# Reordering the steps of a hand-scheduled attention stage ahead of a mixture of experts

## The chip, the cores and the metric

The kernel runs on one core of a Trainium2 chip. The metric is the device time of one execution in microseconds (us); lower is better. The engines are named as in the profile: PE multiplies matrices (PEld is its weight load), DVE and ACT work element by element, POOL issues the indirect transfers, SP issues most of the others.

## The reference, cut to what matters

```python
f = 1.0 / (1.0 + np.exp(-f_logit))               # (4, 8, 768, 48): batch, heads, time, width
for t in range(768):
    state = f[:, :, t, :, None] * state + k[t] (outer) v[t]      # 48 x 48 per batch and head
    y[:, :, t] = q[t] @ state
x = y as (3072 tokens, 384)
g = argmax(x @ w_group);  e = argmax(x @ w_expert[g])            # 4 groups of 4 experts
out = softmax weight of g * softmax weight of e * (relu(x @ w1[g, e]) @ w2[g, e])   # F = 1024
```

Each token goes to one of 16 experts. All numbers are fp32.

## The kernel before, in words

The time axis is cut into 6 chunks of 128 steps, each chunk into 2 **units** of two batches: unit i = (chunk i // 2, half s = i % 2), 12 units (NU). Inside a chunk the recurrence is done by matrix products. A unit goes through **stages**, each a Python generator whose pieces end at a `yield`; the letter is the one that the written order uses:

- c `bounded` (L519): DVE keeps the logits f above -44.
- g `gated`: ACT computes Exp and Ln of f (L529, L530; one piece), then for each of the two batches PE forms the running sums `cs` by a triangular matrix (L536) and ACT makes `eq` and `kh` from them (L537, L538); the last row of `eq`, the chunk's decay, is copied to the tile `ends` by a transfer that ACT issues (L543).
- m `multiplied`: DVE multiplies q by eq (L551) and k by kh (L554).
- t `turned`: PE transposes q and k (L566), ACT copies them out (L567); a fifth piece, in odd units, transposes `ends` to `gt` on PE (L573), and ACT copies that to `decays` (L574).
- s `scored`: PE computes the scores `ap` (L587), DVE masks them to `am` (L590).
- n `stated`: PE computes the state's increment `ds` (L604); in a second piece DVE adds it to the state and multiplies by the decays (L610, L611).
- w `weighed`: PE multiplies q by the state (L626); second piece: the scores by v (L631), and ACT copies the outputs to `xT` (L634).
- d `done`: PE forms the router's logits `lT`, ACT copies them (L646, L648); second piece: PE turns them (`lg`, L651), DVE copies them (L652); after an odd unit the routing of the chunk starts.
- x `listed`: two pieces transpose the outputs (`x_ps`, L666) and copy them (L667), a third issues their store to `x_dram` from ACT's queue (L669).
- r is a slot for one piece of the routing (`route`): the first two find the best group and expert (ranks, DVE), the third counts tokens per expert on PE (`rk`, L204), the fourth takes each token's place from it (pick, L213 to L216), the next three prepare tables and weights, then PE makes a table of tokens by place (`tb`, L251) and DVE adds it up (L255). After chunk 3 `ranking` (L270 to L283) also picks the two early experts, whose weights are loaded and whose tokens are fetched at once. After chunk 5 it ranks all 16.
- e is a slot for one piece of the early experts' work (`early`): transposing their tokens (L399), 8 pieces of their first layer (L409), 2 of their second (L431).
- l loads the inputs of a unit: SP issues four transfers of 384 KB (L513).

The order on PE, DVE and ACT is the order in which the pieces are issued, written out by hand: a list BEGIN for the first units, then one list per **step** i from 3 on (EVEN or ODD, or one of ORDERS), where `t` is unit i, `g+1` unit i + 1, `d-2` unit i - 2. A piece that a generator no longer has is skipped. SP and POOL are ordered by a planner. Input tiles of f and k have 2 buffers, qh 3, v 4; all products share 8 PSUM banks.

After step NU, 14 main passes of up to 230 tokens and, first and last, one of 128 run their two layers on PE (`turn_in` L399, `up` L409, `down` L438, `turn_out` L447), each with 3 MB of weights; DVE and ACT copy, POOL fetches the tokens (L386) and scatters the results (L423).

Of the kernel before, what the change touches and what calls it, by code (L numbers as in the profile page):

```python
# [22 lines left out]
def kernel(  # L23
# [12 lines left out]
    nc = tc.nc  # L36
# [42 lines left out]
    def bank(shape, name):  # L79
        return ps.tile(shape, FP32, tag="bank", name=name)  # L80
# [98 lines left out]
    def route(c, lg, sb, tabled=True, tidy=None, ranking=None):  # L179
# [68 lines left out]
        if tabled:  # L248
            tb = bank([P, 2, GE, 2], "tb")
            for b in range(B):  # L250
                nc.tensor.matmul(tb.rearrange("p m e j -> p m (e j)"), lhsT=ln[:, b], rhs=val[:, :, b, :], start=(b == 0), stop=(b == B - 1))  # L251
            if ranking:
                ranking(sb)
                yield
            nc.vector.tensor_tensor(table, table, tb, OP.add)  # L255
# [209 lines left out]
    with ExitStack() as fast:  # L465
# [27 lines left out]
        NU = len(units)  # L493
# [28 lines left out]
        def gated(i):  # L522

            c, s = units[i]
            w = live[i]

            nl = w["f"].rearrange("p b h d -> p b (h d)")
            for b in parts(i):
                nc.scalar.activation(nl[:, b], nl[:, b], AF.Exp, bias=0.0, scale=-1.0)  # L529
                nc.scalar.activation(nl[:, b], nl[:, b], AF.Ln, bias=1.0, scale=1.0)  # L530
            eq, qh, kh = pads["eq"][i % 2], w["qh"], pads["kh"][i % 3]
            w.update(eq=eq, kh=kh)
            yield
            for b in range(2):
                cs = bank([P, H, D], "cs")
                nc.tensor.matmul(cs.rearrange("t h d -> t (h d)"), lhsT=tri, rhs=nl[:, b], start=True, stop=True)  # L536
                nc.scalar.activation(eq[:, b, :, 0:D], cs, AF.Exp, bias=0.0, scale=-1.0)  # L537
                nc.scalar.activation(kh[:, b, :, 0:D], cs, AF.Exp, bias=0.0, scale=1.0)  # L538
                if b:

                    if s == 0:
                        ends[c] = sb.tile([B, H * DP], FP32, tag="ends", bufs=1, name="ends")
                    nc.scalar.dma_start(out=ends[c][2 * s:2 * s + 2, :], in_=eq[P - 1:P].rearrange("o b h d -> o b (h d)"))  # L543
                yield
# [12 lines left out]
        def turned(i):  # L557
            w = live[i]
            w["g"] = decays[:, units[i][0], :, 2 * units[i][1]:2 * units[i][1] + 2].rearrange("p a b -> p b a")
            for nm in ("q", "k"):  # L560
                w["T" + nm] = sb.tile([P, 2, HP, P], FP32, tag="T" + nm, name="T" + nm)
            for b in range(2):
                for nm in ("q", "k"):
                    pt = bank([P, HP, P], "tr_" + nm)
                    for a in range(HP):
                        nc.tensor.transpose(out=pt[:, a, :], in_=w[nm + "h"][:, b, 2 * a:2 * a + 2, :].rearrange("t r d -> t (r d)"), identity=ident)  # L566
                    (nc.vector.tensor_copy if i == 0 and nm == "k" else nc.scalar.copy)(w["T" + nm][:, b], pt)  # L567
                    yield
            c, s = units[i]
            if s:  # L570
                gt = bank([P, HP, B], "gt")
                for a in range(HP):
                    nc.tensor.transpose(out=gt[:, a, :], in_=ends[c][:, a * P:(a + 1) * P], identity=ident[0:B, 0:B])  # L573
                nc.scalar.copy(decays[:, c], gt)  # L574
            yield
# [108 lines left out]
        def advance(gens):  # L684
# [5 lines left out]

        STAGES = {"c": bounded, "g": gated, "m": multiplied, "t": turned, "s": scored, "n": stated, "w": weighed, "d": done, "x": listed}
        BEGIN = """c0 g0 p g0 g0 m0 m0 m0 m0 l2 t0 t0 t0 t0 c1 g1 s0 s0 s0 s0 g1 g1 p w0 w0 n0 m1 m1 m1 m1 l3 h x0 x0 x0
            t1 t1 t1 t1 t1 c2 g2 s1 s1 s1 s1 p d0 g2 g2 n0 n1 w1 w1 m2 m2 l4 n1
            d0 x1 x1 x1 t2 t2 t2 t2 c3 g3 s2 s2 s2 s2 g3 g3 w2 d1 w2 n2 m3 m3""".split()
        BEGUN = 3
        EVEN = "l+2 d-2 r r r x-1 x-1 x-1 t t t t g+1 g+1 r n-1 c+2 s s s s w g+2 d-1 w n m+1 m+1".split()
        ODD = "l+2 d-2 r r x-1 x-1 x-1 t t t t g+1 g+1 t r n-1 c+2 r s s s s w g+2 d-1 w n m+1 m+1 n".split()

        ORDERS = {
            4: "l+2 d-2 r r r x-1 x-1 x-1 t t t t g+1 g+1 r n-1 s s s s w d-1 w n m+1 m+1 c+2 g+2".split(),
            5: "l+2 d-2 r r x-1 x-1 x-1 t t t t g+1 g+1 t r n-1 r s s s s w d-1 w n m+1 m+1 n c+2 g+2".split(),
            3: "l+2 d-2 r r x-1 x-1 x-1 t t t t c+1 g+1 g+1 g+1 t r n-1 r s s s s w d-1 w n m+1 m+1 n c+2 g+2".split(),
            NU - 2: "d-2 r r r x-1 x-1 x-1 t t t t g+1 g+1 r n-1 s s s s w d-1 w r n m+1 m+1".split(),
            NU: "d-2 e r r x-1 x-1 x-1 d-1 d-1 r r r e r e r r r r e e e r r e e e r e e".split(),
        }
        steps_of = {}

# [187 lines left out]
    with tc.If(more > 0), ExitStack() as late:  # L897
# [5 lines left out]
        with tc.For_i(0, last, 1) as i:  # L903
            w1, w2 = load_weights(wp, b_expert[0:1, bass.ds(i, 1)])
# [13 lines left out]
            w = fetch(ep, row, P)  # L918
# [32 lines left out]
```

## Time and profile before

| | us |
|---|---|
| runs: median of 3 (lowest to highest) | 466.87 (464.18 to 467.26) |
| the profiled execution | 463.0 |
| its span, first to last instruction | 461.1 |
| PE busy | 433.4 (94% of the span) |
| DVE busy | 175.5 (38%) |
| ACT busy | 122.4 (27%) |
| POOL busy | 74.7 (16%) |

The granted clock of PE is 0.995 of full speed over the span. Busy time of PE counts the modelled ends of pipelined matmuls. Attention and routing fill the first 160 us or so, the experts the rest; the shares above are means over both.

### The profile page before, as it was taken

What the parts mean: (1) busy time and instruction counts of PE and PEld (TensorE: products, weight loads), DVE (VectorE), ACT (ScalarE), POOL (GpSimd) and SP (SyncE); (2) the same over time, 40 slices, a digit from 0 to 9 for tenths busy, and PEclk for the clock granted to TensorE, in tenths of its full rate; (3) what the DMA queues carried; (4) which work ended last, traced back from release to release, by engine and by line L of the source; (5) the groups of instructions that cost most, each with busy time, mean ns of one, the idle gap of its engine ahead of it and who ended that gap; (6) DMA issues with size and microseconds to landing.
All of it is one profiled execution on the core that took longest, in us unless ns stands there. A gap on an engine that the chain in (4) does not pass through costs nothing.

```text
span 461.1 us, 9310 instructions
## 1 busy us (share of the span) xinstructions
PE 433.4 (94%) x3875; PEld 401.5 (87%) x3875; DVE 175.5 (38%) x464; ACT 122.4 (27%) x265; POOL 74.7 (16%) x107
## 2 busy tenths in 40 slices
PE   4999799899999999999999999999999999999991
PEld 2888678788888886989999999999999999999980
DVE  6665474758588670211047121120220221122110
ACT  5565466566655321000101101001011001001000
POOL 3000000000002007311022131312122211120120
PEclk9999999999999999999999999999999999999998
DMA  9999999997706919977538367376486486464100
GB/s 167 174 197 202 202 200 186 194 173 142 138 36 217 390 48 328 309 278 283 174 127 299 102 244 246 110 296 217 128 305 211 137 300 233 129 253 146 42 29 17
DMA packets 136187, 87.71 MB, mean 190 GB/s; under 512 B 106692, under 2 KB 127258, under 8 KB 136138
## 3 DMA queue, kind: packets, MB, share of 16 engines
q1 hardware_dynamic: 126754, 72.38, 60.0%
q0 software_dynamic: 6016, 9.87, 6.6%
q10 hardware_dynamic: 3368, 4.80, 3.2%
q8 instruction: 32, 0.52, 0.5%
q14 instruction: 17, 0.14, 0.1%
HBM read 77.50 MB, written 9.83 MB: 189 GB/s over the span
## 4 chain that ended last, share of the span: by engine, by line
PE 80%; DVE 7%; ACT 5%; DMA 3%; issue 1%; SPq 1%; ACTq 0%; POOL 0%; POOLq 0%; DVEq 0%
PE hp L409 29%; PE yo L438 25%; PE yo L431 4%; PE y L631 4%; DVE am L590 3%; PE ap L587 2%; PE xg_ps L399 2%; PE y_ps L447 2%; PE cs L536 2%; PE ds L604 2%; PE x_ps L666 2%; PE tr_k L566 1%; DMA ld_k<-in_k_dram 1%; PE lT L646 1%; DMA x_dram<-blank 1%
## 5 line engine op out<-in xcount | busy, mean ns | idle before, releaser
L409 PE MATMUL hp<-xe,w 128*128 128x128 f32 (+14 forms) x864 | 138.8, 320 | 1.5 <-issue 0.8
L409 PEld LDWEIGHTS hp<-xe,w 128*128 128x128 f32 x864 | 135.7, 190 | 2.5 <-issue 1.0
L438 PE MATMUL yo<-h,w 128*128 128x230 f32 (+13 forms) x672 | 116.9, 334 | 0.0
L438 PEld LDWEIGHTS yo<-h,w 128*128 128x128 f32 x672 | 113.0, 190 | 0.5
L411 DVE TENSOR_SCALAR h<-hp 128x256 f32<-128x256 f32 (+14 forms) x32 | 17.8, 556 | 129.7 <-PE hp L409 129.7
L423 POOL DMA_INDIRECT out_dram<-yt,xg x32 | 34.6, 1081 | 168.5 <-DVE yt L422 112.4
L439 ACT COPY yT<-yo 128x230 f32<-128x230 f32 (+13 forms) x28 | 9.1, 327 | 145.9 <-PE yo L438 145.9
L413 ACT ACTIVATE h<-hp 128x256 f32<-128x256 f32 (+14 forms) x40 | 18.8, 469 | 102.5 <-PE hp L409 102.5
L386 POOL DMA_INDIRECT xg<-x_dram,rows_p x30 | 32.3, 1078 | 70.2 <-DVE rows_p L322 25.0
L590 DVE TENSOR_TENSOR am<-ap,tri 128x512 f32<-128x512 f32 x48 | 29.8, 681 | 6.1 <-PE ap L587 6.0
L536 PE MATMUL cs<-ld_f,tri 128*128 128x384 f32 x48 | 19.5, 532 | 10.6 <-ACT ld_f L530 10.6
L439 DVE COPY yT<-yo 128x230 f32<-128x230 f32 (+13 forms) x14 | 5.1, 367 | 62.9 <-issue 38.9
L631 PE MATMUL y<-am,v 128*64 128x128 f32 x384 | 26.1, 276 | 2.8 <-DVE am L590 2.7
L631 PEld LDWEIGHTS y<-am,v 128*64 128x64 f32 x384 | 22.1, 137 | 5.7 <-DVE am L590 5.0
L587 PE MATMUL ap<-Tq,Tk 48*128 48x128 f32 x384 | 25.0, 280 | 1.6 <-ACT Tk L567 1.5
L587 PEld LDWEIGHTS ap<-Tq,Tk 48*128 48x128 f32 x384 | 22.7, 187 | 2.7 <-ACT Tk L567 2.0
L536 PEld LDWEIGHTS cs<-ld_f,tri 128*128 128x128 f32 x48 | 8.6, 200 | 15.4 <-ACT ld_f L530 6.8
L431 PE MATMUL yo<-w,h 128*128 128x384 f32 x64 | 21.2, 487 | 0.0
L245 POOL COPY meta<-token 128x4 int32<-128x4 int32 x6 | 1.9, 320 | 114.2 <-DMA x_dram<-meta 114.2
L431 PEld LDWEIGHTS yo<-w,h 128*128 128x128 f32 x64 | 11.9, 190 | 7.7
L634 ACT COPY xT<-y 128x512 f32<-128x512 f32 x24 | 12.9, 589 | 20.7 <-PE y L631 20.7
L422 DVE TENSOR_SCALAR yt<-y_ps,xg 128x384 f32<-128x384 f32 (+14 forms) x28 | 15.8, 606 | 6.4 <-PE y_ps L447 6.4
(166 smaller groups left out, 428.9 us busy)
## 6 DMA issues: line engine op xcount, KB each, us to landing
w<-in_moe_w_dram SPq DMA_DIRECT2D x34, 1536.0 KB, 9.5
qh<-in_q_dram SPq DMA_DIRECT2D x12, 384.0 KB, 6.4
ld_k<-in_k_dram SPq DMA_DIRECT2D x12, 384.0 KB, 6.7
v<-in_v_dram SPq DMA_DIRECT2D x12, 384.0 KB, 6.6
x_dram<-x ACTq DMA_DIRECT2D x12, 384.0 KB, 5.0
ld_f<-in_f_logit_dram SPq DMA_DIRECT2D x11, 384.0 KB, 5.4
out_dram<-yt,xg POOLq DMA_INDIRECT x32, 3.8
xg<-x_dram,rows_p POOLq DMA_INDIRECT x30, 6.9
```

The source lines that it names most:

```text
L386: nc.gpsimd.indirect_dma_start(out=w["x"][0:m, j, :], out_offset=None, in_=x_dram[0:1 + top, :], in_offset=bass.IndirectOffsetOnAxis(ap=ro ...
L409: nc.tensor.matmul(hp[:, o, :], lhsT=w1[:, ko, (f + o) * P:(f + o + 1) * P], rhs=w["xT"][:, ko, :], start=(ko == 0), stop=(ko == KO - 1))
L411: nc.vector.tensor_scalar(h[:, f:f + 2, :], hp, 0.0, None, OP.max)
L413: nc.scalar.activation(h[:, f:f + 2, :], hp, AF.Relu)
L422: nc.vector.tensor_scalar(y[0:m], yp[0:m], w["x"][0:m, j, DM:DM + 1], None, OP.mult)
L423: nc.gpsimd.indirect_dma_start(out=out, out_offset=bass.IndirectOffsetOnAxis(ap=w["x"][0:m, j, DM + 1:RW].bitcast(U32), axis=0), in_=y[0:m ...
L431: nc.tensor.matmul(yp, lhsT=w["h"][:, fo, :], rhs=w2[:, fo, :], start=(fo == 0), stop=(fo == FO - 1))
L438: nc.tensor.matmul(yp, lhsT=w2[:, fo, m * P:(m + 1) * P], rhs=w["h"][:, fo, :], start=(fo == 0), stop=(fo == FO - 1))
L536: nc.tensor.matmul(cs.rearrange("t h d -> t (h d)"), lhsT=tri, rhs=nl[:, b], start=True, stop=True)
L587: nc.tensor.matmul(ap[r][:, a, :], lhsT=w["Tk"][rows, b, a, :], rhs=w["Tq"][rows, b, a, :], start=True, stop=True)
L590: nc.vector.tensor_tensor(am[:, r], ap[r], tri.unsqueeze(1).broadcast_to((P, HP, P)), OP.mult)
L631: nc.tensor.matmul(ys[r][DP * b:DP * b + DP, a, :], lhsT=w["v"][:, b, 2 * a + r, :], rhs=w["am"][b][:, r, a, :], start=(c == 0 and a == 0) ...
```

## The change

Most of it is in the written order. The fifth piece of `turned` becomes a stage of its own, b (`decayed`), and stands at the begin of odd steps, followed by the second piece of n of the unit before. The bound c+2 stands behind the scores' masks. Exp and Ln become two pieces (for units after the first): Exp stands behind lT's copy, Ln behind the copies of the outputs. The third piece of x, the store, stands behind the running sums of the next unit. In odd steps the fourth r stands at the end. The orders of steps 3, 4 and 5 are dropped, so that these follow ODD and EVEN, and BEGIN ends with c4, Exp and Ln of unit 4. `ranking` has a piece of its own, and the slots of steps 10 and 12 are rearranged for it. One copy of turned keys in unit 0 goes from DVE to ACT.

```diff
--- before.py
+++ after.py
@@ -250,6 +250,7 @@
             for b in range(B):
                 nc.tensor.matmul(tb.rearrange("p m e j -> p m (e j)"), lhsT=ln[:, b], rhs=val[:, :, b, :], start=(b == 0), stop=(b == B - 1))
             if ranking:
+                yield
                 ranking(sb)
                 yield
             nc.vector.tensor_tensor(table, table, tb, OP.add)
@@ -527,6 +528,8 @@
             nl = w["f"].rearrange("p b h d -> p b (h d)")
             for b in parts(i):
                 nc.scalar.activation(nl[:, b], nl[:, b], AF.Exp, bias=0.0, scale=-1.0)
+                if i:
+                    yield
                 nc.scalar.activation(nl[:, b], nl[:, b], AF.Ln, bias=1.0, scale=1.0)
             eq, qh, kh = pads["eq"][i % 2], w["qh"], pads["kh"][i % 3]
             w.update(eq=eq, kh=kh)
@@ -564,8 +567,11 @@
                     pt = bank([P, HP, P], "tr_" + nm)
                     for a in range(HP):
                         nc.tensor.transpose(out=pt[:, a, :], in_=w[nm + "h"][:, b, 2 * a:2 * a + 2, :].rearrange("t r d -> t (r d)"), identity=ident)
-                    (nc.vector.tensor_copy if i == 0 and nm == "k" else nc.scalar.copy)(w["T" + nm][:, b], pt)
+                    (nc.vector.tensor_copy if i == 0 and b == 0 and nm == "k" else nc.scalar.copy)(w["T" + nm][:, b], pt)
                     yield
+
+        def decayed(i):
+
             c, s = units[i]
             if s:
                 gt = bank([P, HP, B], "gt")
@@ -690,20 +696,16 @@
 
 
 
-        STAGES = {"c": bounded, "g": gated, "m": multiplied, "t": turned, "s": scored, "n": stated, "w": weighed, "d": done, "x": listed}
-        BEGIN = """c0 g0 p g0 g0 m0 m0 m0 m0 l2 t0 t0 t0 t0 c1 g1 s0 s0 s0 s0 g1 g1 p w0 w0 n0 m1 m1 m1 m1 l3 h x0 x0 x0
-            t1 t1 t1 t1 t1 c2 g2 s1 s1 s1 s1 p d0 g2 g2 n0 n1 w1 w1 m2 m2 l4 n1
-            d0 x1 x1 x1 t2 t2 t2 t2 c3 g3 s2 s2 s2 s2 g3 g3 w2 d1 w2 n2 m3 m3""".split()
+        STAGES = {"c": bounded, "g": gated, "m": multiplied, "t": turned, "s": scored, "n": stated, "w": weighed, "d": done, "x": listed, "b": decayed}
+        BEGIN = """c0 g0 p g0 g0 m0 m0 m0 m0 l2 t0 t0 t0 t0 c1 g1 g1 s0 s0 s0 s0 g1 g1 p w0 w0 n0 m1 m1 m1 m1 l3 h x0 x0 x0
+            t1 t1 t1 t1 b1 c2 g2 g2 s1 s1 s1 s1 p d0 g2 g2 n0 n1 w1 w1 m2 m2 l4 n1
+            d0 x1 x1 t2 t2 t2 t2 c3 g3 g3 x1 s2 s2 s2 s2 g3 g3 w2 d1 w2 n2 m3 m3 c4 g4 g4""".split()
         BEGUN = 3
-        EVEN = "l+2 d-2 r r r x-1 x-1 x-1 t t t t g+1 g+1 r n-1 c+2 s s s s w g+2 d-1 w n m+1 m+1".split()
-        ODD = "l+2 d-2 r r x-1 x-1 x-1 t t t t g+1 g+1 t r n-1 c+2 r s s s s w g+2 d-1 w n m+1 m+1 n".split()
-
+        EVEN = "l+2 d-2 n-1 r r r x-1 x-1 t t t t g+1 g+1 x-1 r s s s s c+2 w d-1 g+2 w g+2 n m+1 m+1".split()
+        ODD = "l+2 d-2 b n-1 r r x-1 x-1 t t t t g+1 g+1 x-1 r s s s s c+2 w d-1 g+2 w g+2 n m+1 m+1 r n".split()
         ORDERS = {
-            4: "l+2 d-2 r r r x-1 x-1 x-1 t t t t g+1 g+1 r n-1 s s s s w d-1 w n m+1 m+1 c+2 g+2".split(),
-            5: "l+2 d-2 r r x-1 x-1 x-1 t t t t g+1 g+1 t r n-1 r s s s s w d-1 w n m+1 m+1 n c+2 g+2".split(),
-            3: "l+2 d-2 r r x-1 x-1 x-1 t t t t c+1 g+1 g+1 g+1 t r n-1 r s s s s w d-1 w n m+1 m+1 n c+2 g+2".split(),
-            NU - 2: "d-2 r r r x-1 x-1 x-1 t t t t g+1 g+1 r n-1 s s s s w d-1 w r n m+1 m+1".split(),
-            NU: "d-2 e r r x-1 x-1 x-1 d-1 d-1 r r r e r e r r r r e e e r r e e e r e e".split(),
+            NU - 2: "d-2 r r r x-1 x-1 t t t t g+1 g+1 x-1 r s s s s w d-1 w n m+1 m+1 r r".split(),
+            NU: "d-2 e r r d-1 x-1 x-1 d-1 x-1 r r r e r e e r r r r e e r r e e e r r e e".split(),
         }
         steps_of = {}
```

## Rows read from the trace of the kernel before

**Rows 1.** Windows, main passes: stretch, length, busy time and instructions of each engine, clock, DMA.

```profile
181.03:441.66 260.63, 258.92 (x1592) 254.10 (x1591) 56.92 (x126) 24.64 (x59) 57.31 (x53) 1.00 0.60 207
```

**Rows 2.** Windows of units 7, 8 and 11, and the sum of units 2 to 11.

```profile
97.89:111.05 13.16, 12.36 (x192) 10.67 (x191) 8.29 (x20) 7.89 (x18) 0.00 (x0) 1.00 0.79 145
111.05:122.15 11.10, 11.10 (x180) 10.08 (x179) 8.74 (x27) 7.53 (x16) 0.66 (x1) 1.00 1.09 189
...
146.72:155.30 8.58, 8.58 (x147) 7.90 (x146) 5.17 (x18) 3.57 (x10) 1.17 (x2) 1.00 1.04 387
sum 123.57, PE 114.75 PEld 100.28 DVE 81.24 ACT 72.13 POOL 3.93; mean PE 11.47 PEld 10.03 DVE 8.12 ACT 7.21 POOL 0.39
```

**Rows 3.** Waits, 0 to 215 us: us in total, times, longest us.

```profile
DVE st L611 <- ACT decays L574: 17.4, 4, 5.9
```

**Rows 4.** Timeline of step 7: start, us, engine, line, operation, count, [idle before <- releaser].

```profile
103.10 0.56 DVE L611 TENSOR_TENSOR st<-sp,decays 128x384 f32<-128x384 f32 x1 [3.61 <-ACT decays L574]
...
104.77 2.48 DVE L590 TENSOR_TENSOR am<-ap,tri 128x512 f32<-128x512 f32 x4
...
106.70 0.44 PE L631 MATMUL y<-am,v 128*64 128x128 f32 x4 [0.65 <-DVE am L590]
```

**Rows 5.** Timeline of PE in steps 7 and 8.

```profile
101.03 0.41 PE L573 MATMUL gt<-ident,ends 4*128 4x4 f32 x4
...
101.73 2.06 PE L587 MATMUL ap<-Tq,Tk 48*128 48x128 f32 x32
...
114.08 0.28 PE L251 MATMUL tb<-val,ln 128*128 128x64 bf16 x4
114.30 2.06 PE L587 MATMUL ap<-Tq,Tk 48*128 48x128 f32 x32
...
118.24 1.92 PE L631 MATMUL y<-am,v 128*64 128x128 f32 x32
119.98 1.09 PE L604 MATMUL ds<-v,kh 128*64 128x48 f32 x32
121.00 0.42 PE L651 MATMUL lg<-fold,lgT 128*128 128x40 f32 x2
```

**Rows 6.** Timeline of SP's queue: the loads of f of units 4 and 7.

```profile
34.10 2.86 SPq L513 DMA_DIRECT2D ld_f<-in_f_logit_dram  x1
...
70.95 0.50 SPq L513 DMA_DIRECT2D ld_f<-in_f_logit_dram  x1
```

**Rows 7.** Tile ld_f, 34 to 35 us: from the issue at 34.10 to landing.

```profile
DMA to landing us min/median/max: 8.3/8.3/8.3
```

**Rows 8.** DMA issues of the page: KB each, median us to landing.

```profile
ld_f<-in_f_logit_dram SPq DMA_DIRECT2D x11, 384.0 KB, 5.4
```

**Rows 9.** DMA, 34 to 90 us.

```profile
DMA packets 49839, 10.88 MB, mean 194 GB/s; under 512 B 48800, under 2 KB 49824, under 8 KB 49832
```

**Rows 10.** Timeline of ACT's queue in step 8.

```profile
115.41 0.61 ACTq L543 DMA_DIRECT2D ends<-eq  x1
```

**Rows 11.** DMA, 28.1 to 31 us: ACT's queue (q10), packets, MB, share.

```profile
q10 hardware_dynamic: 4, 0.00, 0.5%
```

**Rows 12.** Timeline of steps 10 to 12: ranking, early fetch, ranks of chunk 4.

```profile
138.94 0.17 DVE L270 TENSOR_TENSOR rkey<-run,base 128x16 f32<-128x16 f32 x1
...
144.31 0.17 DVE L313 CAST rows_e<-got 128x2 uint32<-128x2 f32 x1
...
145.27 0.95 DVE L554 SCALAR_TENSOR_TENSOR kh<-kh,ld_k 128x768 f32<-128x768 f32 x1
...
146.68 0.94 POOL L386 DMA_INDIRECT xg<-x_dram,rows_e  x1 [0.30 <-issue]
...
148.90 0.20 PE L204 MATMUL rk<-ohe,strictb 128*128 128x64 bf16 x1
...
155.30 0.85 PE L399 MATMUL xg_ps<-ident,xg 128*128 128x128 f32 x6
```

**Rows 13.** Tile xg, 146.5 to 147 us: from the issue at 146.68 to landing.

```profile
DMA to landing us min/median/max: 7.5/7.5/7.5
```

## The prediction

> **What bounds the kernel now.** I read the windows by stage first. From 181.03 us, where the main expert passes begin, PE is busy 258.92 of 260.63 us [rows 1]: a row of dense matmuls that starts when the stages before it let it. What can be won lies before. Next I cut the attention stage at the first transposition of each unit [rows 2]. The ten stretches, from 31.73 to 155.30 us, last 123.57 in sum and are far from equal: unit 8 takes 11.10 us with PE busy all of it, unit 7 takes 13.16 (unit 9 too). The reader is to see the same work at different lengths: PE waits inside the long ones, although its busy share is above 90%.
>
> The waits [rows 3] and the timeline of step 7 [rows 4] name the main reason. DVE sits 17.4 us in four waits for `decays`. In step 7 its state update runs at 103.10 after 3.61 us of such waiting; the bound of f, pick and the masks are queued behind it, so the masks start only at 104.77, although half of the scores, begun at 101.73 [rows 5], were there a microsecond later. PE reaches the output products and stops for the masks at 106.70. Steps 3, 4 and 5 have orders of their own in which bound, Exp and Ln of a later unit stand late, in step 3 just ahead of the running sums that need them.
>
> **The change part by part.** *Lengths without a wait* [rows 5]. An even unit without a stall is 11.10. In it the table product takes 0.22 (114.08 to 114.30) and the state product 1.02 (119.98 to 121.00); in an odd step `gt` and `rk` take 0.70 together (101.03 to 101.73), half each. With `gt` at the begin of the odd step, ahead of the transposed outputs, it falls into the stretch before. So, if nothing waits: unit 2, which has no table product, 11.10 - 0.22 + 0.35 = 11.23; the odd units 3 to 9, with `rk` in its stead, 11.10 - 0.22 + 0.35 = 11.23 (four: 44.92); units 4, 6, 8 11.10 + 0.35 = 11.45 (34.35); unit 10, without state product, 11.45 - 1.02 = 10.43; unit 11 8.58 - 0.35 = 8.23. Sum 109.16 against 123.57: **14.4 us** are there to be won.
>
> *Decays and states at the begin.* The state update then needs the logits' copy, `gt` and one small copy, all at hand early in the odd step; the ranks follow on DVE and end before PE comes to `rk`. The masks can start with the first half of the scores, near 115.3 in the clock of unit 8, and take 2.48 us [rows 4], to 117.8: 0.4 ahead of the output products at 118.24 [rows 5]. The stops of rows 4 are gone; that is in the 14.4. Late next would be the masks themselves, by 0.4 us less than anything that delays them.
>
> *Bounds behind masks, Exp and Ln around the outputs' copies.* DVE does the bound when the masks are done. Exp sits between lgT and the outputs' copies, while ACT waits for the output products anyway; Ln sits where ACT waited for the transposed outputs. With these covers they cost nothing. A new wait is made, though: if f has not landed, DVE holds the bound (qh and kh of the next unit are queued behind it), ACT holds Exp, and behind Exp stand the outputs' copies, for which PE waits at the begin of the next step. Without the covers, late f is late PE. In step 2 unit 3's Exp and Ln stay where they are, right before the sums: I keep 0.5 us of waiting there.
>
> *f is wanted earlier* for units 4 to 7. Loads run at 194 GB/s in these steps [rows 9], 2.0 us for each 384 KB. Landing takes 5.4 us in the median [rows 8], 8.3 for unit 4's [rows 7]. Unit 4's f is issued at 34.10 [rows 6], there at 42.4, and wanted about 8.4 us after the step's first transposition at 31.73, near 40.1. What DVE and ACT can't absorb of the 2.3 I put at 0.8 us of PE. Unit 7's is issued at 70.95, there at 76.4. Step 5 would begin at 31.73 + 11.23 + 11.23 + 11.45 + 1.3 (the two waits so far) = 66.9 and want it at 75.3; 0.2 is absorbed: 0.9. Units 5, 6 and 8 are just in time; with 8.3 us of landing each they would add 3.5, kept for the range. SP's queue isn't reordered by hand; its loads start when buffers come free, none later than now.
>
> The Trainium skill, "DMA: Bandwidth & Descriptors", section Specifications, gives a core about 358 GB/s of HBM; by it neither load would be late, and the sum would end 1.7 us lower. The row says 194, with 48800 of 49839 packets under 512 B, and the same section asks for at least 512 B for line rate: the measurement decides.
>
> *The outputs' store behind the sums.* On ACT's own queue `ends` now passes the store, except in step 2. ACT's issue leaves the place ahead of the turned copies, which come earlier; nothing on PE. `ends` was issued at 115.41 [rows 10]; the new `gt` stands behind lg, at 121.00 + 0.25: 5.8 us later. With the loads at full rate, the four packets of an `ends` issued at 28.13 were through by 31 [rows 11], 2.9 us. I take no wait; the bounds are 0 and, with the 8.3 of a large load, 2.5 us in each odd step.
>
> *Slots (ranking, pick) behind products.* Pick leaves the place ahead of the masks in odd steps. In step 10 the ranking leaves it too, where it began at 138.94 [rows 12]. It now follows kh(11): the early experts' row list, at 144.31, comes behind two products of 0.95 more and the masks' own wait for scores, about 2.5 us later, with PE 1.3 us earlier. Two things are then late. The ranks of chunk 4, next on DVE, hold `rk` (now 148.90) for some 1.4. The second early fetch, issued at 146.68 and there 7.5 later [rows 13], 154.2, was 1.1 ahead of its transposition at 155.30, and now holds PE for 1.1. Together 2.5, bounds 0 and 4. The expert weights are issued behind the ranking, later by as much, and needed only after that. In the last step the early experts' work fills PE up to the main passes, and the chain of ranks and fetch beside it moves along: 0, bounds -0.5 and +1.5. A copy of turned keys goes to ACT in unit 0, where loads set the pace: 0.
>
> *Sum.* 14.4 - 0.5 - 0.8 - 0.9 - 2.5 = **9.7 us**. The profiled execution took 463.0 (span 461.1), so 453.3 in its own terms; the median of the runs is 466.87, all three above the profiled one, and against that the forecast is **457.2**.
>
> **The rivals.** *Loads bind*: f lands 8.3 us after its issue in every early step, or one more 384 KB load gets ahead of it in SP's order, 2.0 us. A lag is paid once: 3.5 to 5.5, so 460.7 to 462.7. For it: loads run without a pause through these steps. Against: a unit's four loads and its store, 1.97 MB, need 10.1 us at 194 GB/s and a step 11.3, so the lag can't grow.
>
> *Banks*: `rk` now keeps one of the eight PSUM banks until pick, after the masks and kh. If each new bank on PE then waits for a copy, 0.5 to 1.5 us in five odd steps, 2 to 7 of the gain are left, about 462: the order is rewritten and the waits change their names. Against: the state product's bank is given back earlier.
>
> *Slower*: `gt` at the begin of an odd step holds all of PE until `ends` has landed. The wait is landing - 5.8 us in four steps and landing - 4.3 in step 3, where the sums come later; from a landing of 7.4 us on it eats the gain, and at the 8.3 of rows 7 it costs 14: 471. Against: the 2.9 of rows 11. By the page named above, section Queues, rings and completion order (the Trainium skill), each DMA engine takes packets from the queues in turn, so 4 KB on ACT's would not stand behind SP's loads, and this rival's price would be nothing; that agrees with rows 11.
>
> **How the numbers follow.** Chances: forecast 0.57, loads 0.16, banks 0.14, slower 0.13. 1% of 466.87 is 4.7 us, about what a measurement here can tell from no change: faster is below 462.2, slower above 471.5. Nearly all of the forecast, over half of loads and a third of banks are faster: 0.69. Most of the last rival is slower: 0.11; the rest, 0.20, is within. The range goes from 452, where nearly all of the 14.4 are won, to 467, which takes in loads and banks; the forecast's own range is 453 to 461.
>
> **What would show it.** Stretches of units 4 to 9 at 11.2 to 11.5; no wait of DVE for `decays` above 1 us; masks that follow the first scores; output products without a stop; Ln inside ACT's wait for the transposed outputs. The forecast is wrong if PE waits for `ends` at `gt`, if DVE waits for f beyond unit 7, or if the main passes begin less than 6 us ahead of 181.03.

## The result and the profile after

The changed kernel takes **452.29 us** (median of 4 runs, 451.6 to 453.47); the kernel before takes 466.96 beside it (464.18 to 467.26). The ratio is 0.970 [0.966, 0.974]: 3.0% faster, 14.7 us between the medians. The profiled execution took 451.6 us (span 449.7, mean clock 0.992), 11.4 less than that of before. A ratio compares undisturbed executions only, so for a kernel that changes how often the clock drops it can stand nearer to 1 than its medians do.

The page's shares of the span say that PE is now nearly all of it; in the chain of waits DVE fell to 2%, from 7% before, and PE rose from 80% to 88%:

```profile
PE 429.3 (95%) x3875; PEld 400.8 (89%) x3875; DVE 174.4 (39%) x463; ACT 122.0 (27%) x266; POOL 73.7 (16%) x107
...
PE 88%; DMA 4%; DVE 2%; issue 2%; ACT 2%; POOL 0%; SPq 0%; POOLq 0%; DVEq 0%
```

The windows of the changed kernel, cut at the first transposition of each unit (columns as in rows 1 and 2; the lines are units 2 and 3, 7 and 8, 10 and 11, the sum of units 2 to 11, and the main passes):

```profile
31.19:43.37 12.18, 11.73 (x181) 10.27 (x180) 6.00 (x10) 8.01 (x16) 0.00 (x0) 1.00 1.18 207
43.37:54.76 11.39, 11.39 (x187) 10.18 (x186) 7.94 (x20) 8.58 (x20) 0.00 (x0) 1.00 1.12 197
...
89.15:100.41 11.26, 11.26 (x188) 10.27 (x186) 7.84 (x20) 7.57 (x17) 0.19 (x1) 1.00 1.14 200
100.41:111.98 11.57, 11.57 (x185) 10.48 (x184) 9.18 (x27) 7.46 (x17) 0.00 (x0) 1.00 1.09 180
...
123.23:133.88 10.65, 10.65 (x152) 9.45 (x151) 9.27 (x30) 5.89 (x15) 0.00 (x0) 1.00 0.13 39
133.88:143.16 9.28, 8.32 (x144) 7.60 (x142) 6.38 (x26) 3.47 (x9) 2.29 (x3) 1.00 0.78 277
sum 111.97, PE 110.56 PEld 99.72 DVE 81.04 ACT 71.11 POOL 2.90; mean PE 11.06 PEld 9.97 DVE 8.10 ACT 7.11 POOL 0.29
...
169.63:430.26 260.63, 258.93 (x1592) 254.12 (x1591) 56.94 (x126) 24.60 (x59) 58.00 (x54) 1.00 0.60 208
```

Against rows 2 the ten stretches give 123.57 - 111.97 = 11.60. Units 3 to 10 run without a stop of PE (length equal to PE's busy time): odd units in 11.25 to 11.39, even ones in 11.57, where before unit 7 took 13.16. Unit 8, dense before too, is 0.47 longer: it now holds `gt`. The first unit cut starts 0.54 earlier (31.73 to 31.19); from the early experts' first transposition to the main passes it takes 26.47 instead of 25.73, 0.74 lost; the main passes are the same to 0.01. 11.60 + 0.54 - 0.74 = 11.40, the whole difference of the spans.

Step 7 after (timeline; start, us, engine, line, operation, [idle before <- releaser]) answers to rows 4 and 5:

```profile
88.76 0.56 DVE L617 TENSOR_TENSOR st<-sp,decays 128x384 f32<-128x384 f32 x1
...
92.55 2.06 PE L593 MATMUL ap<-Tq,Tk 48*128 48x128 f32 x32
...
93.74 2.48 DVE L596 TENSOR_TENSOR am<-ap,tri 128x512 f32<-128x512 f32 x4 [2.92 <-PE ap L593]
...
96.14 0.55 DVE L520 TENSOR_SCALAR ld_f<-ld_f 128x768 f32<-128x768 f32 x1
...
96.49 1.92 PE L637 MATMUL y<-am,v 128*64 128x128 f32 x32
...
96.87 0.85 ACT L530 ACTIVATE ld_f<-ld_f 128x768 f32<-128x768 f32 x1
...
98.24 1.07 ACT L640 COPY xT<-y 128x512 f32<-128x512 f32 x2 [0.52 <-PE y L637]
...
99.19 0.86 ACT L533 ACTIVATE ld_f<-ld_f 128x768 f32<-128x768 f32 x1
```

The state update begins at 88.76, ahead of the step's first transposition at 89.15, without a wait for `decays`; DVE then waits 2.92 us for the scores, so the masks begin 1.2 after the scores (3.04 before) and the output products run in one piece. Exp and Ln lie on either side of the outputs' copies.

What is left of waits, 0 to 215 us (us in total, times, longest us; the 5.2 of cs is the kernel's start):

```profile
DVE am L596 <- PE ap L593: 16.6, 12, 2.9
...
DVE ld_f L520 <- DMA ld_f<-in_f_logit_dram: 9.8, 7, 2.7
...
PE cs L539 <- ACT ld_f L533: 5.9, 3, 5.2
...
DVE st L617 <- ACT decays L580: 1.3, 1, 1.3
...
PE xg_ps L400 <- DMA xg<-x_dram,rows_e: 1.1, 1, 1.1
```

The 17.4 us of DVE's waits for `decays` [rows 3] have become 1.3, in step 3. DVE waits for f seven times, in six units (two halves of unit 0, then units 2, 3, 4, 5 and 8, the last for 0.47 us), yet PE hardly pays for it. The two stops of PE that the forecast named around the ranking are there (timeline):

```profile
136.75 0.20 PE L204 MATMUL rk<-ohe,strictb 128*128 128x64 bf16 x1 [0.96 <-ACT dl L208]
...
144.78 0.52 PE L400 MATMUL xg_ps<-ident,xg 128*128 128x128 f32 x3 [1.09 <-DMA xg<-x_dram,rows_e]
```

### The profile page after: what moved, and what is told of

Read it like the earlier page. It is cut to its first block, busy times and chain, and to the rows that moved or that the text cites. A ratio compares the mean times of both kernels' runs of the same rounds, so it can differ in the third digit from the quotient of the medians.

```text
span 449.7 us, 9297 instructions
## 1 busy us (share of the span) xinstructions
PE 429.3 (95%) x3875; PEld 400.8 (89%) x3875; DVE 174.4 (39%) x463; ACT 122.0 (27%) x266; POOL 73.7 (16%) x107
## 4 chain that ended last, share of the span: by engine, by line
PE 88%; DMA 4%; DVE 2%; issue 2%; ACT 2%; POOL 0%; SPq 0%; POOLq 0%; DVEq 0%
PE hp L410 30%; PE yo L439 26%; PE yo L432 5%; PE y L637 4%; PE ap L593 4%; PE cs L539 3%; PE lT L652 2%; PE x_ps L672 2%; PE ds L610 2%; PE xg_ps L400 2%; PE y_ps L448 2%; PE y L632 2%; DMA xg<-x_dram,rows_e 2%; PE tr_k L569 2%; PE tr_q L569 2%
## 5 line engine op out<-in xcount | busy, mean ns | idle before, releaser
L539 PE MATMUL cs<-ld_f,tri 128*128 128x384 f32 x48 | 19.2, 526 | 5.9 <-ACT ld_f L533 5.9
L637 PE MATMUL y<-am,v 128*64 128x128 f32 x384 | 23.1, 273 | 0.0
L401 DVE COPY xe<-xg_ps 128x384 f32<-128x384 f32 (+14 forms) x30 | 12.8, 463 | 8.8 <-PE xg_ps L400 8.8
```

Source lines behind the costliest of these rows:

```text
L637: nc.tensor.matmul(ys[r][DP * b:DP * b + DP, a, :], lhsT=w["v"][:, b, 2 * a + r, :], rhs=w["am"][b][:, r, a, :], start=(c == 0 and a == 0) ...
```

## The experiments

Three groups of runs, each on a chip of its own beside the kernel before: 467.0 us in the first, 470.74 in the second, 471.12 in the third. Only runs of one group are compared in us.

**First group: the changed kernel, and one part of it undone at a time.**

*e0_after*, the changed kernel again, no edit.

> The changed kernel itself, on the chip of the next three, as their yardstick. The profiled executions of the two kernels are 11.4 us apart (463.0 and 451.6), the medians 14.7 (466.96 and 452.29). If the removed waits of PE are all of it, the two kernels stay 11 to 15 us apart here, 452 against 463 to 467, and the spread of the kernel before is that of its own load-dependent waits; if half of the distance was a chip's, they come nearer than 10.

453.06 us (451.6 to 454.86), ratio 0.972 [0.967, 0.976]. It repeats: the two kernels are 13.9 us apart, within the 11 to 15 that were expected. The clocks differ too: seven of the eleven executions of before have a mean clock of 0.983, and none of these six is under 0.988. Its profiled execution was the slowest of six, and its windows of units 6 and 7 (the last three columns are clock, DMA share, GB/s) and timeline show why (timeline in the second block):

```profile
77.41:90.76 13.35, 11.72 (x185) 10.47 (x183) 9.19 (x26) 6.85 (x15) 0.00 (x0) 1.00 1.17 191
90.76:103.68 12.92, 12.92 (x187) 11.93 (x186) 8.23 (x20) 8.31 (x19) 0.19 (x1) 0.87 1.21 199
```

```profile
87.81 0.56 DVE L520 TENSOR_SCALAR ld_f<-ld_f 128x768 f32<-128x768 f32 x1 [3.48 <-DMA ld_f<-in_f_logit_dram]
...
88.41 0.84 ACT L530 ACTIVATE ld_f<-ld_f 128x768 f32<-128x768 f32 x1 [2.27 <-DVE ld_f L520]
...
89.16 1.05 ACT L640 COPY xT<-y 128x512 f32<-128x512 f32 x2
...
89.78 1.14 PE L672 MATMUL x_ps<-ident,xT 128*128 128x128 f32 x8 [1.59 <-ACT xT L640]
```

That is the chain that the prediction described, once: f of unit 8 is late, DVE holds the bound, ACT holds Exp, the outputs' copy stands behind Exp, PE waits 1.59 us. In the next stretch the granted clock is 0.87 and the same work takes 12.92 instead of 11.26. One late load cost 1.8 + 1.7 us.

*e1_late_decays*: decays and state update of odd steps back behind the running sums.

```diff
-        ODD = "l+2 d-2 b n-1 r r x-1 x-1 t t t t g+1 g+1 x-1 r s s s s ...
+        ODD = "l+2 d-2 r r x-1 x-1 t t t t g+1 g+1 b x-1 r n-1 s s s s ...
```

> The changed kernel with decays and the state's update put back behind the running sums in odd steps; bounds, Exp, Ln, pick and ranking stay in their new places. Theory (three things stood ahead of the masks in DVE's queue: the update, 6.4 us into the odd step, then the bound, 0.5, then pick, 0.75): the update alone lets the masks start at 6.9 instead of 8.0 us into the step, and the output products stop for 0.4 to 0.8 us in steps 5, 7 and 9 only: 453.5 to 455. Rival (the decays' place is the whole gain of the odd steps): all of 1.6 us per odd step comes back, 457 to 459. Rival (the decays' place does nothing): 452.

453.76 us (453.18 to 455.97), ratio 0.975 [0.970, 0.980]: 0.7 us between the medians. Windows of units 3, 7 and 8:

```profile
43.12:56.98 13.86, 12.63 (x192) 10.64 (x191) 8.10 (x20) 8.77 (x20) 0.00 (x0) 1.00 1.22 199
90.89:102.59 11.70, 11.70 (x191) 10.51 (x190) 8.27 (x20) 7.75 (x18) 0.19 (x1) 1.00 1.05 177
102.59:113.70 11.11, 11.11 (x181) 10.09 (x179) 8.76 (x27) 7.30 (x16) 0.00 (x0) 1.00 1.21 209
```

Units 7 and 8 together take 22.81, against 22.83 in the changed kernel: nothing is lost there, `gt` only changes its stretch. Yet DVE waits for `decays` almost as long as before (14.9 us in 4 waits): with the bound behind the masks, the wait delays the masks too little to matter, as in step 7 here: update at 95.62, masks at 96.09, outputs at 98.67 without a stop. Only step 3 pays, where the copy of `decays` came at 50.02 and the masks stopped PE twice. So the size was met, but from one step and not from all four.

*e2_early_bounds*: bounds ahead of the masks again, Exp and Ln together.

```diff
-        EVEN = "... x-1 r s s s s c+2 w d-1 g+2 w g+2 n m+1 m+1".split()
+        EVEN = "... x-1 r c+2 s s s s w g+2 g+2 d-1 w n m+1 m+1".split()
         (the same exchange in ODD)
```

> The changed kernel with the bound ahead of the masks and Exp and Ln together ahead of lT's copy, as in the ordinary steps of before; decays stay early. Theory: with the decays early the masks have 2.9 us of slack in odd steps and 0.6 in even ones, so a bound of 0.5 ahead of them costs nothing, and Exp and Ln fill a time in which ACT waits anyway: 452 to 453. Rival (Exp and Ln around the outputs' copies are what removes waits): 1 us per step, 458 to 462. Since f is wanted some 3 us earlier, units 4 to 8 may wait for their loads: up to 2 us, 454.

455.44 us (454.35 to 456.76), ratio 0.978 [0.973, 0.982]: 2.4 us more than the changed kernel. The theory (no cost) failed, and the part about late f came, larger than its 2 us. Again all of it is step 3, where f of unit 5 has not landed when the bound comes up; the other stretches are those of the changed kernel (11.25 and 11.57). Window of step 3, then PE's timeline in it:

```profile
43.32:59.50 16.18, 13.68 (x188) 11.64 (x187) 8.41 (x21) 9.06 (x20) 0.00 (x0) 0.89 1.26 194
```

```profile
52.74 0.43 PE L637 MATMUL y<-am,v 128*64 128x128 f32 x2 [1.37 <-DVE am L596]
53.93 3.46 PE L637 MATMUL y<-am,v 128*64 128x128 f32 x29 [0.76 <-DVE am L596]
```

Of the 4.8 us above the changed kernel's 11.39, 2.1 are these two waits and 1.7 the clock behind them: the 29 products of 53.93 take 3.46 us, where 32 take 1.92 at full clock. The last 1.0 lies in neither. Not each of its executions had this: mean clocks go from 0.988, the traced one, to 0.995.

*e3_early_rank*: in step 10 the slot of the ranking ahead of the scores again.

```diff
-            NU - 2: "... g+1 g+1 x-1 r s s s s w d-1 w n m+1 m+1 r r".split(),
+            NU - 2: "... g+1 g+1 x-1 r r s s s s w d-1 w r n m+1 m+1".split(),
```

> The changed kernel with the ranking after chunk 3 back ahead of the masks of step 10, and the early fetch's list right behind the second piece of w. Theory: the two waits that moving it made (0.96 us of rk, 1.09 of the early tokens' transposition) go, and the output products of step 10 stop for the masks again for 0.8 to 1.0: 451 to 452.3, no more than 1 us faster. Rival (the hand-over to the experts hangs on this list): 2 us faster, 450. Rival (the stop in step 10 was the dearer one): 454.

450.8 us (449.88 to 452.05), ratio 0.968 [0.964, 0.973]: 2.3 us faster than the changed kernel by the medians, **the best of the versions on this chip, ahead of both kernels**. The theory allowed 1 us; the size is that of the first rival, the hand-over to the experts. Windows of unit 10, unit 11 and the stage up to the main passes, and then, from PE's timeline, `rk` and the early fetch's transposition:

```profile
123.37:134.88 11.51, 11.31 (x153) 9.63 (x152) 10.66 (x38) 5.89 (x15) 1.74 (x2) 1.00 0.43 135
134.88:143.01 8.13, 8.13 (x143) 7.63 (x142) 4.93 (x18) 3.46 (x9) 1.07 (x2) 1.00 1.04 393
143.01:168.20 25.19, 24.86 (x182) 20.05 (x182) 13.47 (x56) 6.48 (x17) 5.77 (x6) 1.00 0.62 225
```

```profile
136.62 0.19 PE L204 MATMUL rk<-ohe,strictb 128*128 128x64 bf16 x1
...
143.01 0.85 PE L400 MATMUL xg_ps<-ident,xg 128*128 128x128 f32 x6
```

Both stops are gone. The three stretches take 44.83 against 10.65 + 9.28 + 26.47 = 46.40: 1.6 of the 2.3 us are seen in the traces, the rest is open.

**Second group: one part alone on the order of before.**

*e4_decays_alone*: stage b, and the state update with it, at the begin of odd steps; nothing else.

```diff
-        ODD = "l+2 d-2 r r x-1 x-1 x-1 t t t t g+1 g+1 t r n-1 c+2 r s s s s w g+2 ...
+        ODD = "l+2 d-2 b n-1 r r x-1 x-1 x-1 t t t t g+1 g+1 r c+2 r s s s s w g+2 ...
         (the same move in the orders of steps 3 and 5)
```

> The kernel before with only the decays and the state's update put at the begin of odd steps (also in its own orders of steps 3 and 5). Theory: in steps 7 and 9 any one of the three things ahead of the masks can be taken away and the output products find their masks in time; so the decays alone win 1.3 to 1.6 us in each of these two steps and up to 1 in steps 3 and 5, 4 to 5 in all: 462 to 463 against 467. Rival (the gain needs the moves together): within 1.5 us of the kernel before. Steps 3 to 6 keep their waits for Exp and Ln.

461.69 us (460.39 to 469.0), ratio 0.982 [0.978, 0.985]: about 9 us less, twice what was expected. Windows of units 4, 5 and 7:

```profile
64.89:77.95 13.06, 11.99 (x185) 10.59 (x184) 9.36 (x27) 8.90 (x18) 0.38 (x1) 1.00 0.96 164
77.95:89.20 11.25, 11.25 (x187) 10.25 (x186) 7.85 (x19) 6.09 (x16) 0.00 (x0) 1.00 0.93 166
102.26:113.52 11.26, 11.26 (x188) 10.27 (x187) 7.94 (x20) 7.70 (x17) 0.00 (x0) 1.00 0.90 168
```

Steps 5, 7 and 9 are as dense as in the changed kernel, by this part alone. 13.34 + 13.16 + 13.16 - 3 x 11.25 = 5.9, less some 0.47 in each even unit, is the 4 to 5 that were expected. The other half does not come from these stretches. Five of its seven executions (460.4 to 463.3 us) have a mean clock of 0.986 to 0.992, those of before on this chip 0.977 to 0.988; the traced one is one of the two at 0.975, and its step 3 takes 19.17 us at 0.73, so the half that the clock gave back is seen in the clocks and not in a trace.

*e6_masks_first_alone*: in ODD alone the bound and pick behind the masks; with the bound, Exp and Ln go behind lT's copy.

```diff
-        ODD = "... g+1 g+1 t r n-1 c+2 r s s s s w g+2 d-1 w n m+1 m+1 n".split()
+        ODD = "... g+1 g+1 t r n-1 s s s s c+2 w d-1 g+2 w n m+1 m+1 r n".split()
```

> The kernel before with only the bound and pick moved behind the masks, in the ordinary odd steps (7, 9 and 11); decays late, orders of steps 3 to 5 as before. Theory: as good as the decays in steps 7 and 9, 1.3 to 1.6 us each, and nothing elsewhere: 463.5 to 465 against 467. Rival (late decays alone hold the masks): less than 1 us.

468.51 us (462.79 to 470.29), ratio 0.994 [0.991, 0.998]: 2.2 us between the medians. ODD serves steps 7 and 9 only here, and unit 7 takes 11.95 with PE busy throughout, 1.2 less than before, and unit 8 11.11 as before (windows of unit 7 and of step 3, then PE's timeline in step 3):

```profile
101.90:113.85 11.95, 11.95 (x191) 10.68 (x190) 8.10 (x20) 7.76 (x18) 0.00 (x0) 1.00 0.80 147
...
43.95:63.44 19.49, 16.56 (x191) 14.34 (x190) 8.45 (x20) 7.74 (x17) 0.00 (x0) 0.74 1.36 191
```

```profile
48.79 2.15 PE L536 MATMUL cs<-ld_f,tri 128*128 128x384 f32 x4 [2.93 <-ACT ld_f L530]
...
51.80 3.79 PE L587 MATMUL ap<-Tq,Tk 48*128 48x128 f32 x32
```

Its trace brought the surprise: step 3, whose order this edit does not touch, takes 19.49 us at a granted clock of 0.74. The scores there last 3.79 us instead of the 2.06 of rows 5.

*e7_before*: the kernel before once more, to see step 3.

> The kernel before once more, for a trace of another execution. Its executions so far fall into three groups: 467 us at a mean granted clock of 0.983, 464.5 at 0.988 to 0.992, 462.9 at 0.992 to 0.995, and the trace read for the prediction is of the last. If this one falls into the first, the trace should show a stretch of the attention stage at the lower clock that the other trace does not have, behind one of PE's waits; theory: behind the 2.9 us in step 3, which the change removes. If it falls into the last, it shows nothing new.

468.01 us, clock 0.985. Window of step 3 and PE's timeline at its running sums; the two blocks after them are the same two views of the first trace of before, which the prediction was read from:

```profile
44.18:60.86 16.68, 13.75 (x192) 11.39 (x191) 8.28 (x20) 7.74 (x17) 0.00 (x0) 0.90 1.36 195
```

```profile
49.01 2.91 PE L536 MATMUL cs<-ld_f,tri 128*128 128x384 f32 x4 [2.93 <-ACT ld_f L530]
```

```profile
43.96:59.37 15.41, 12.39 (x191) 10.71 (x190) 8.28 (x20) 7.63 (x17) 0.00 (x0) 1.00 1.33 194
```

```profile
48.80 1.56 PE L536 MATMUL cs<-ld_f,tri 128*128 128x384 f32 x4 [2.93 <-ACT ld_f L530]
```

PE stands still for the same 2.93 us in both. Then the same four products take 1.56 us in the one and 2.91 in the other: the granted clock fell towards the lower of its two levels (1.2 of 2.4 GHz) in one execution and not in the other. The stretch lasts 15.41, 16.68 or (e6) 19.49 us: 0, 1.3 or 4.1 more. The executions of the kernel before in the first group lie at 462.8 and 462.9 (mean clock 0.992 and 0.995), at 464.1 and 464.6 (0.992, 0.988), and from 466.9 on (seven of eleven, all at 0.983): the same steps. In the second group most lie near 470.8 at 0.977 to 0.981, 2.8 above this execution, as the 19.49 are above its 16.68. The trace that the prediction was read from (463.0, 0.995) is of the fastest kind, the median of the slowest.

*b_f_three*: e3 with a third buffer for f.

```diff
-   tile([P, 2, H, D], FP32, tag="ld_" + nm, name="ld_" + nm)
+   tile([P, 2, H, D], FP32, tag="ld_" + nm, bufs=3 if nm == "f" else 2, name="ld_" + nm)
```

> The changed kernel with the ranking of step 10 back ahead of the masks (as in the run that did only that) and a third buffer for the tile of f, by which SP's order puts the loads of f of units 7 to 9 ahead of one load of 384 KB each. Theory: loads of f that land late in some executions (PE 1.6 us idle behind one of them in the trace of the repeated run, and a stretch at a clock of 0.87 after it) go, so the slower executions go: 450 median and a spread under 1.5 us, 2 to 3 us below the changed kernel. Rival (f is bound by the bytes ahead of it in any order): as the run with the ranking alone, 450.8 with 2 us of spread; the load that f now passes is late instead.

455.6 us (454.55 to 456.28), ratio 0.968 [0.965, 0.971], e3's own ratio of the first group. A gain over e3 and a spread under 1.5 us were expected; the ratio is the same and the spread 1.7. In the trace DVE no longer waits for f of units 5 and 8, as it does in e3 for 0.25 and 0.82 us, but PE did not stand behind those waits. So the buffer bought nothing that can be measured; e3 itself was not run on this chip.

**Third group: step 3, the store and the copy.**

*e10_unit4_early*: the kernel before, with unit 4's bound, Exp and Ln at the end of BEGIN, as the change has them, and out of step 3.

```diff
-            d0 x1 x1 x1 t2 ... n2 m3 m3""".split()
+            d0 x1 x1 x1 t2 ... n2 m3 m3 c4 g4""".split()
-            3: "... t t t t c+1 g+1 g+1 g+1 t r n-1 ...
+            3: "... t t t t g+1 g+1 t r n-1 ...
```

> The kernel before with one thing changed: bound, Exp and Ln of unit 4 at the end of step 2 instead of inside step 3; all else as before, the late decays too. Theory: PE's wait of 2.9 us in step 3 falls to under 1, and with it goes the stretch at the lower clock that follows it in most executions (3.8 to 4.1 us where the step runs at 0.73 or 0.74, 1.3 at 0.90): 5 to 7 us in the median, ratio 0.985 to 0.990, no execution with a mean clock under 0.985. Rival (the clock falls for another reason, or falls elsewhere instead): only the 2.5 us of waiting go, ratio 0.994, and the low clocks stay.

466.42 us (464.59 to 467.43), 4.7 less than before between the medians; ratio 0.995 [0.991, 0.998]. Step 3:

```profile
44.00:57.61 13.61, 12.56 (x191) 10.64 (x190) 7.81 (x19) 6.55 (x16) 0.00 (x0) 1.00 1.27 195
```

The wait for Exp and Ln is gone, 15.41 (first chip) became 13.61, and all 12 executions have a mean clock of 0.986 to 0.992, where 10 of the 17 of before have 0.975 to 0.979, at 471.0 to 472.9 us. Of the 4.7 us, 1.8 is the shorter stretch; the other 2.9 its trace at full clock doesn't show, and I put them down to the drops that no longer come. The forecast was 5 to 7 us and a ratio of 0.985 to 0.990: the ratio is the rival's 0.994, but the low clocks that the rival kept are gone.

*e11_unit4_late*: the changed kernel with the reverse edit.

```diff
-            d0 x1 x1 t2 ... n2 m3 m3 c4 g4 g4""".split()
+            d0 x1 x1 t2 ... n2 m3 m3""".split()
+            3: "l+2 d-2 b n-1 r r x-1 x-1 t t t t c+1 g+1 g+1 g+1 g+1 x-1 r s s s s ...
```

> The changed kernel with bound, Exp and Ln of unit 4 put back into step 3, ahead of the sums, as before; everything else new. Theory: the wait of 2 to 3 us comes back in step 3, and in most executions the lower clock behind it: 3 to 7 us slower than the changed kernel, ratio to the kernel before 0.978 to 0.987 where the changed kernel had 0.9715. Rival (once the decays are early, step 3 has slack for it): ratio 0.972 to 0.975.

460.29 us (458.63 to 460.84), ratio 0.983 [0.978, 0.988]. Step 3 takes 13.96 us, and the wait is back:

```profile
43.20:57.16 13.96, 11.52 (x187) 10.28 (x186) 8.31 (x21) 9.23 (x19) 0.00 (x0) 1.00 1.11 196
```

```profile
47.55 1.56 PE L539 MATMUL cs<-ld_f,tri 128*128 128x384 f32 x4 [2.44 <-ACT ld_f L533]
```

That is 2.1 to 2.6 us above the two other variants of the changed kernel in this group, about the wait. The clock stayed at 1.00 behind it: a wait of 2.44 us did not bring the drop in this execution. Nor do the others show it: a stretch of 19.2 us at 0.73 takes 0.011 off the mean clock of 466 us, and these six executions have 0.984 to 0.989, e9's 0.985 to 0.988. So the ratio came out as forecast by the wait alone, and the half of the theory that brought the lower clock back failed.

*e9_store_first*: the outputs' store ahead of `t` again, so that `ends` stands behind it on ACT's queue.

```diff
-        ODD = "l+2 d-2 b n-1 r r x-1 x-1 t t t t g+1 g+1 x-1 r s s s s ...
+        ODD = "l+2 d-2 b n-1 r r x-1 x-1 x-1 t t t t g+1 g+1 r s s s s ...
         (the same move in BEGIN, EVEN and NU - 2)
```

> The changed kernel with the store of the outputs issued where it was, ahead of the turned copies, so that `ends` stands behind 384 KB in ACT's queue in every step. Theory: `ends` still lands before gt, which comes 5.4 us or more after its issue, and ACT's 0.4 us of issue have slack: ratio 0.971 to 0.974, gt without a wait. Rival (`ends` lands behind the store, and the early gt holds all of PE): 1 to 2.5 us in each odd step, ratio 0.98 to 0.995.

458.15 us (456.46 to 459.77), ratio 0.978 [0.973, 0.983]. The ratio lies between the theory's 0.974 and the rival's 0.980; the trace decides for the theory: `gt` waits for nothing in this order either (timeline of step 2's end):

```profile
43.95 0.42 PE L657 MATMUL lg<-fold,lgT 128*128 128x40 f32 x2
44.30 0.41 PE L579 MATMUL gt<-ident,ends 4*128 4x4 f32 x4
```

The odd stretches are the 11.25 of the changed kernel. Whether the store's move is worth anything is not settled: against the one execution of e12 the difference is 0.5 us.

*e12_keys_dve*: the changed kernel with unit 0's second copy of turned keys on DVE again.

```diff
-  (nc.vector.tensor_copy if i == 0 and b == 0 and nm == "k" else nc.scalar.copy)(w["T" + nm][:, b], pt)
+  (nc.vector.tensor_copy if i == 0 and nm == "k" else nc.scalar.copy)(w["T" + nm][:, b], pt)
```

> The changed kernel with the second copy of turned keys of unit 0 back on DVE. One look: the first transposition of unit 2 was at 31.73 us before and at 31.19 after, of which the prediction took nothing. Theory: that copy is the cause (DVE does it ahead of unit 1's bound), so it comes back to 31.6 to 31.8. Rival (the loads set the pace there, and the half microsecond is chance): 31.2.

457.64 us, one execution. Unit 2 starts at 31.73, as in the kernel before, against 31.19 after and 31.02 in e11. But b_f_three, which has the copy on ACT, also starts at 31.73, and e9 at 32.89: the 0.54 may be the copy or the start's scatter. Over all traces, six of the eight with that copy on ACT start unit 2 at 31.02 to 31.40, and none of the six with it on DVE before 31.73. That speaks for the copy; one execution of each doesn't show it.

## Why the prediction was right, and where it was not

The median of 452.29 is 4.9 us under the forecast of 457.2. It lies 0.7 below the forecast's own range of 453 to 461 and only 0.3 inside the whole range, whose lower end stood for winning nearly all of the 14.4. That end was reached in part by another way, told below, so it is luck that the range held. Of the signs of being wrong one did come: DVE waits for f of unit 8, 0.47 us in the profiled execution and 3.48 in e0's. And one wait of DVE for `decays`, 1.3 us in step 3, is above the 1 us named. The other two signs of being wrong did not come: PE waits for `ends` nowhere, and the main passes begin 11.4 us ahead of 181.03.

*Lengths without a wait: right.* Odd units were put at 11.23 and came at 11.25 to 11.39, even ones at 11.45 and came at 11.57. `gt` costs an even stretch 0.12 more than half of the 0.70 in rows 5. The sum is 111.97 against 109.16: 0.95 of the 2.81 is unit 2 (0.45 of it the wait for unit 3's Ln, forecast 0.5; the other half is no wait, as PE is busy 11.73 there for the 11.23), 1.05 unit 11, 0.22 unit 10, the rest small.

*Decays and states, bounds behind masks: right in sum, not in how it is shared.* The prediction gave the dense odd steps mostly to the early decays. e4 shows that decays alone do all of it in steps 5, 7 and 9; e6 shows that the masks' place alone does nearly as much in steps 7 and 9. For this, units 7 and 8 must be taken together, as 0.47 of unit 7's 1.9 us only moves with `gt` into unit 8: the pair takes 24.26 us before, 22.83 in the changed kernel and in e4, 23.06 in e6, so 1.2 of 1.4. e1 shows that with the masks first the decays' place is worth nothing in these steps. Each takes something away from ahead of the masks on DVE, and either is enough: in e1 the masks run from 96.09 to 98.57, and the output products begin at 98.67. The gains don't add. In step 3, where `decays` and f are both late, both are needed (e1 and e2 each lose there alone).

*f is wanted earlier: over-sized.* 0.8 and 0.9 us were set down for units 4 and 7. Unit 4's f is as late as forecast: DVE waits 2.40 us for it, for the 2.3 of the sum. But DVE and ACT absorb all of that, and PE doesn't stop. Unit 7's is not late: DVE doesn't wait for it. The sum had kept its issue at 70.95 while the step that needs it moved forward; SP issued it at 68.51. The third buffer (b_f_three) gains nothing. It was not that loads ran faster: units 2 to 8 moved 180 to 207 GB/s, as the 194 of rows 9. None of these stretches reaches the 358 GB/s that the Trainium skill gives ("DMA: Bandwidth & Descriptors", Specifications). Unit 11's, in which 75 of 1667 packets are under 512 B, moved 387 before [rows 2], above that figure. The chain exists, though: e0's profiled execution shows it in unit 8, at 3.5 us with what the clock did after it. That is the rival *loads bind*, in single executions and not in the median.

*The ranking: right.* `rk` 0.96 for 1.4, the early fetch 1.09 for 1.1. e3 takes this part back and wins 2.3 us, against the 2.5 of the forecast: this part of the change is a loss. What the later ranking gains in unit 10 (10.65 against 11.51 in e3) comes back as the longer unit 11 and stage behind it.

*Unit 0's copy and the last step, both put at 0:* the start came 0.54 earlier (cause open), the last stage lost 0.74, inside its -0.5 to +1.5 but mostly the 1.09 of the fetch again (in e2's trace, where PE doesn't wait for the early tokens, the stage takes 25.72 us as before).

By its own terms the forecast was 9.7 us; the profiled executions differ by 11.4. The 1.7 between them: f +1.7, the start +0.5, `rk` +0.4, the last stage +0.4 (1.1 forecast, 0.7 lost), less 0.5 in unit 2 and 0.9 in the small excess of the other stretches. All but the first nearly cancel, so it is the term for f that is left.

*What went wrong is the last step of the sum*: the gain was taken from one execution and set against the median. 466.96 is 4.0 above the profiled execution of before; 452.29 is 0.7 above that of after. 11.4 + 4.0 - 0.7 = 14.7. The prediction noted that all runs lay above the profiled one, but let that offset stand on both sides. e7 and e6 show an offset of this kind: behind the 2.93 us wait of step 3 the clock falls in some executions. e10 shows that taking that wait away, and nothing else, ends the long executions; the changed kernel takes it away too. The reverse doesn't hold: e11 puts a wait of 2.44 us back into the changed kernel, and the drops don't come back. That the 467 us executions of the first chip are those with the full drop is inferred, from the matching steps (0, 1.3, 4.1) and from the clock: 0.983 is 0.012 under the 0.995 of the execution traced, about the 0.011 of one full drop. None of them was traced there.

*The rivals.* `gt` waiting for `ends`: PE waits for `ends` in no trace, not even in e9, where it is issued behind the store. On ACT the traces put single waits down to `ends` (4.2 us in e0, ahead of lgT's copy), but PE did not stand behind that one. The rival's last sentence, by the Trainium skill ("DMA: Bandwidth & Descriptors", Queues, rings and completion order), put its price at nothing, and that is what held. Banks: no wait of PE for a copy remains between units 3 and 10. Loads: as above, in f's paragraph.

Open: why one and the same wait brings the drop in some executions only; why only two of e4's seven executions have the clock of a full drop (0.975), though it keeps the wait of 2.93 us, when 11 of the 17 of before beside it are at 0.981 or less; so few executions can be chance.

Open, too, is a second stop with a drop. At the begin of the second main pass PE waits 0.82 us in all six traces of the first group and of the two kernels, and 2.95 to 4.08 in all eight of the second and third group. The clock falls behind each of these eight, to 0.76 to 0.86 over the 48 products that follow, which then take 11.0 to 12.6 us for 9.56 (timelines of PE, before and e12):

```profile
189.26 9.56 PE L409 MATMUL hp<-xe,w 128*128 128x230 f32 x48 [0.82 <-issue]
```

```profile
181.53 11.93 PE L410 MATMUL hp<-xe,w 128*128 128x230 f32 x48 [4.07 <-issue]
```

Wait and clock together cost 3.6 to 5.1 us in the four traces of before and its variants and 5.6 to 6.3 in the four variants of the changed kernel. So this is much of what sets the second and third group apart from the first, and some 1 to 2 us of what the change wins is lost there. The cause of the wait was not found.

## What to carry to other kernels

Where an in-order engine holds several items ahead of the one that PE waits for, count the room: moving any one item may be enough, and the gains of two such moves don't add. Before a gain read from one trace is set against a median, compare the traced execution with the spread of the runs: a stall of some us on PE can cost more than its length (here 0 to 4.1 us more behind one and the same wait), because the clock may fall behind it, and one trace may show no sign of that. Work that feeds an indirect transfer can be worth its place even where an engine is busy: here the ranking's later place paid 0.9 us in one stretch and cost 1.2 and 1.3 in the next two.

## What the runs showed of the hardware

The granted clock fell behind PE's stops in some executions: to 0.90, 0.74 and 0.73 of full speed as a mean of the stretch after a wait of 2.93 us, 0.89 in e2 after waits of 1.37 and 0.76, 0.87 in e0 after one of 1.59, and 0.76 to 0.86 behind the eight waits of 2.95 to 4.08 at the second main pass. In other executions it stayed at 1.00 behind waits of 2.93 (before) and 2.44 (e11). While it was down, the scores took 3.79 us instead of 2.06 (e4 and e6).
